# Two late copies of z, octet 7: GpSimd's queue in place of SyncE's

## The chip, the cores and the metric

The kernel runs on one core of one Trainium2 chip. The metric is device time in microseconds (us) of one execution. "TensorE" is the profile's PE (its weight loads PEld), "VectorE" DVE, "ScalarE" ACT, "GpSimd" POOL, "SyncE" SP.

## The reference

Linear attention (8 batches, 8 heads, 576 positions, head size 64) is followed by a spectral mixing block on the 512 channels:

```python
X = np.fft.rfft(x, axis=1)                      # x: the attention's output, (8, 576, 512)
Xr, Xi = (np.real(X[:, :64]), np.imag(X[:, :64]))
Yr = np.einsum('bmd,mde->bme', Xr, w_r) - np.einsum('bmd,mde->bme', Xi, w_i)
Yi = np.einsum('bmd,mde->bme', Xr, w_i) + np.einsum('bmd,mde->bme', Xi, w_r)
Y[:, :64] = Yr + 1j * Yi
y = np.fft.irfft(Y, n=576, axis=1)
u = x + y
return (u + np.maximum(u @ w_ch, 0.0)).astype(np.float32)
```

The 64 modes have a weight matrix of 512 x 512 each, real and imaginary. They are streamed in eight octets (o = 0 to 7).

## The kernel before

For each octet the kernel forms `yst` (the mixed spectrum) and `zst` (the same times `w_ch`), both 128 x 512 in bf16, and copies them by DMA into tables from which the inverse transform is taken as matmuls. Octets 6 and 7 go into `yl`, the "late" table: 16 rows of it for each copy, y into rows 0 and 64 (plus 16 for octet 7), z into rows 32 and 96.

```python
def put(src, o, dst, copies):
    if o < 7:
        sp.dma_start(dst[16 * o:16 * o + 16], src)
    if o > 5:
        for s in copies:
            r = 32 * s + 16 * (o - 6)
            (pool if o == 6 else sp).dma_start(yl[r:r + 16], src)
...
put(yst, o, yall, (0, 2))
...                                   # transposes, product with w_ch
act.copy(zst[:, cut[0]], pz[0])
dve.tensor_copy(zst[:, cut[1]], pz[1])
put(zst, o, zall, (1, 3))
```

After the last octet the output is summed in 20 steps (`seq`). The first four need only `yst` and `zst`; from step 4 on, matmuls read `yl` ("late"):

```python
def late(self, which):
    if self.early:
        return
    for a, (bp, n) in enumerate(self.items):
        r = 64 * a + 32 * which
        back((self.q if which else self.p)[a], n, bp, CL, yl, slice(r, r + 32), ...)
...
seq[2].relu()
seq[0].store()                        # ofr, 256 KB
seq[1].store()                        # ofr, 256 KB
seq[3].base(1)
seq[3].straight(1)
seq[2].store()                        # of, 512 KB
...
for g in range(3, len(seq)):
    s, ts = seq[g], [seq[i] for i in ahead[g - 3:g - 2]]
    for t in ts:
        t.base(1)
        t.straight(1)
    if g > 3:
        s.base(0)
        s.straight(0)
    for t in ts:
        t.late(1)                     # reads z from yl: the first to wait for the copies
    s.late(0)
    for t in ts:
        t.relu()
    s.store()
```

While a late matmul of TensorE waits for its copy (0.25 us before), no matmul that stands after it in the program is carried out. So a wait of the first `late(1)` holds up what TensorE has to do after it.

Of the kernel before, what the change touches and what calls it, by code (L numbers as in the profile page):

```python
# [43 lines left out]
def kernel(  # L44
# [15 lines left out]
    pool, sp = InOrder(tc, nc.gpsimd), InOrder(tc, nc.sync)  # L60
# [364 lines left out]
    for t in range(3):  # L425
        r = slice(32 * t, 32 * t + 32)
        dve.tensor_scalar_mul(out=minus[r], in0=ident_f[r, r], scalar1=-1.0)
    every = mf[0:96, 0:32]
    for t in range(3):
        r = slice(32 * t, 32 * t + 32)  # L430
# [160 lines left out]
    zall = pw.tile([128, B_, DMODEL], BF16, name="zall", tag="wt")  # L591
    yall = pw.tile([128, B_, DMODEL], BF16, name="yall", tag="wt")
    yl = pw.tile([128, B_, DMODEL], BF16, name="yl", tag="wt")
# [222 lines left out]
# [3 lines that stand above are left out]
        if o > 5:  # L819
            for s in copies:  # L820
                r = 32 * s + 16 * (o - 6)
                (pool if o == 6 else sp).dma_start(yl[r:r + 16], src)


    class Last:
# [97 lines left out]
    while mixq:  # L923
        key = mixq.pop(0)
        g, o, i = key[0], key[1] // 2, key[1] % 2
# [17 lines left out]
        if g == NG - 1 and i == 1:  # L943
# [5 lines left out]
            for h in range(2):  # L949
                dve.tensor_tensor(out=yst[:, H * h:H * h + H], in0=py[:, H * h:H * h + H],  # L950
                                  in1=yacc[:, o, H * h:H * h + H], op=ALU.add)
            put(yst, o, yall, (0, 2))
            if o < 5:
                fill(min(n, 1))
# [23 lines left out]
# [3 lines that stand above are left out]
            fill(max(n - 2, 0) if o < 5 else n)  # L981
        else:
# [70 lines left out]
```

## Time and profile before

| before | us |
|---|---|
| device time at first, median of 3 (range) | 442.57 (441.81 to 443.12) |
| span of the profiled run | 440.2 |
| last mix matmuls begin ("mix" below; the last weight tile landed just before) | 404.17 |
| end of VectorE's part of zst, octet 7 ("zst" below) | 407.66 |
| second late matmul of TensorE begins | 412.13 |
| last sum on VectorE ends | 434.82 |

Two clocks: *after mix* counts from the start of the last mix matmuls, *after zst* from the end of VectorE's `zst`. Before, the second late matmul begins 7.96 us after mix, and the second copy has landed 4.42 us after zst (412.08 - 407.66).

The page's list of DMA issues has one line for each kind of copy (source and destination, queue, count, KB, median us from issue to landing). Those of octet 7 on SyncE:

```profile
yl<-yst SPq DMA_DIRECT2D x2, 128.0 KB, 3.6
yl<-zst SPq DMA_DIRECT2D x2, 128.0 KB, 3.6
```

So a copy lands some 3.6 us after its issue has begun, of which the issue itself takes 0.55 to 0.60.

### The profile page before, as it was taken

The numbers are of one execution on the slowest core, as the hardware profiler recorded it, in microseconds if no ns is written. First come the engines' busy times: TensorE is split into PE (matmuls) and PEld (weight loads), VectorE is DVE, ScalarE is ACT, GpSimd is POOL, SyncE is SP. The second block draws the span as 40 slices with busy tenths as digits, with TensorE's granted clock in tenths as the row PEclk, the third lists the DMA queues.
The fourth block names the chain that finished last, engine by engine and source line by source line (L and its number), as shares of the span: only waits on it lengthen the run. The fifth ranks groups of instructions, "written<-read, shape, count | busy, mean of one in ns | idle before, by whom it ended". The sixth has DMA issues, their size and how long they took to land.

```text
span 440.2 us, 10147 instructions
## 1 busy us (share of the span) xinstructions
PE 337.2 (77%) x4233; PEld 203.5 (46%) x4233; DVE 296.3 (67%) x583; ACT 279.8 (64%) x478; POOL 112.5 (26%) x151
## 2 busy tenths in 40 slices
PE   1677778688688687797796787474679998998993
PEld 0445556455465465464564554252335454333320
DVE  5568686765886876976858878443883334785684
ACT  2787686786987885875857867310644442765772
POOL 6232132113211222221222221121101111682082
PEclk9978796789998896996979988975999999999997
DMA  8999999999999999999999999999999999996787
GB/s 188 211 210 211 235 215 237 231 219 239 236 210 239 221 228 235 237 212 237 228 220 238 210 237 210 238 213 210 212 216 222 222 220 220 209 219 146 251 358 294
DMA packets 51710, 99.55 MB, mean 226 GB/s; under 512 B 2512, under 2 KB 13648, under 8 KB 51664
## 3 DMA queue, kind: packets, MB, share of 16 engines
q0 software_dynamic: 45232, 85.86, 99.5%
q1 hardware_dynamic: 6432, 13.04, 8.5%
q8 instruction: 33, 0.54, 0.4%
q14 instruction: 13, 0.11, 0.1%
HBM read 163.64 MB, written 9.44 MB: 393 GB/s over the span
## 4 chain that ended last, share of the span: by engine, by line
PE 35%; DMA 25%; ACT 17%; DVE 16%; issue 5%; POOL 0%; SPq 0%; ACTq 0%; DVEq 0%; POOLq 0%
PE one L37 14%; DMA wt<-in_moe_w_i_dram 14%; PE pt L37 13%; DMA wt<-in_moe_w_r_dram 8%; ACT AB L37 7%; PE two L37 7%; DVE m L37 5%; DVE mk L37 4%; ACT AQ L37 4%; ACT XT L37 2%; DMA qb<-in_q_dram 2%; PE pp L37 2%; ACT qT L37 1%; DVE xw L37 1%; DVE XT L37 1%
## 5 line engine op out<-in xcount | busy, mean ns | idle before, releaser
L37 ACT ACTIVATE AB<-two 128x1024 bf16<-128x1024 f32 x64 | 62.0, 1026 | 11.1 <-DVE mk L37 7.8
L37 ACT ACTIVATE AQ<-two 128x1024 bf16<-128x1024 f32 x64 | 62.6, 1045 | 1.9 <-PE two L37 1.8
L37 ACT CAST xw<-pt 128x512 bf16<-128x512 f32 x50 | 29.3, 587 | 41.8 <-PE pt L37 41.7
L37 DVE TENSOR_REDUCE m<-two 128x8 f32<-128x1024 f32 x32 | 39.2, 1224 | 15.4 <-PE two L37 15.2
L37 DVE TENSOR_TENSOR va<-vn,ee 128x1152 bf16<-128x1152 f32 x32 | 42.0, 1355 | 6.3 <-DMA vn<-in_v_dram 6.2
L37 DVE TENSOR_REDUCE mk<-two 128x8 f32<-128x1024 f32 x32 | 38.9, 1218 | 9.9 <-PE two L37 9.9
L37 POOL DMA_DIRECT2D wt<-in_moe_w_i_dram x28 | 20.9, 748 | 90.2 <-PE pt L37 36.2
L37 POOL DMA_DIRECT2D wt<-in_moe_w_r_dram x30 | 22.5, 750 | 67.3 <-PE one L37 39.8
L37 PE MATMUL pt<-wchb,xT 128*128 128x512 bf16 x136 | 35.8, 387 | 5.0 <-DVE xT L37 3.8
L37 ACT COPY qT<-one 128x512 bf16<-128x512 bf16 (+1 forms) x32 | 19.5, 641 | 29.4 <-PE one L37 28.9
L37 PE MATMUL two<-w2blk,qT 128*128 128x256 bf16 x128 | 22.2, 302 | 20.0 <-ACT AQ L37 8.4
L37 PEld LDWEIGHTS <-xs 128*128 128x128 bf16 x624 | 31.3, 102 | 12.6 <-issue 7.4
L37 PE MATMUL one<-wt,XT 128*32 128x512 bf16 x304 | 28.3, 464 | 5.2 <-DMA wt<-in_moe_w_i_dram 3.6
L37 PEld LDWEIGHTS <-qT 128*128 128x128 bf16 x144 | 14.7, 104 | 36.8 <-issue 32.9
L37 PE MATMUL two<-qT,w2blk 128*128 128x512 bf16 x64 | 28.0, 438 | 3.6 <-ACT AQ L37 3.5
L37 PEld LDWEIGHTS <-AQ 128*128 128x128 bf16 x512 | 26.6, 114 | 8.7 <-issue 5.4
L37 PE MATMUL one<-kvz,AQ 128*128 128x65 bf16 x512 | 29.2, 216 | 0.9 <-ACT qT L37 0.8
L37 DVE RECIPROCAL rd<-one 128x6 f32<-128x6 f32 x48 | 9.4, 196 | 28.8 <-PE one L37 28.7
L37 DVE COPY xT<-pt 128x512 bf16<-128x512 bf16 x36 | 17.0, 471 | 17.4 <-PE pt L37 17.4
L37 PEld LDWEIGHTS <-XT 128*32 128x32 bf16 x512 | 14.7, 149 | 28.9 <-issue 22.0
L37 PE MATMUL two<-mT,minus 96*128 96x512 bf16 x64 | 28.1, 439 | 0.0
L37 DVE TENSOR_TENSOR xs<-one,rd 128x384 bf16<-128x384 f32 x48 | 26.8, 558 | 1.6
(151 smaller groups left out, 726.9 us busy)
## 6 DMA issues: line engine op xcount, KB each, us to landing
wt<-in_moe_w_r_dram POOLq DMA_DIRECT2D x30, 1024.0 KB, 28.2
wt<-in_moe_w_i_dram POOLq DMA_DIRECT2D x28, 1024.0 KB, 28.7
out_dram<-of SPq DMA_DIRECT2D x16, 512.0 KB, 4.3
vn<-in_v_dram POOLq DMA_DIRECT2D x14, 576.0 KB, 25.0
kb<-in_k_dram POOLq DMA_DIRECT2D x16, 288.0 KB, 21.0
qb<-in_q_dram POOLq DMA_DIRECT2D x16, 288.0 KB, 19.4
xs<-in_moe_w_i_dram POOLq DMA_DIRECT2D x2, 1024.0 KB, 23.7
vn<-in_v_dram SPq DMA_DIRECT2D x2, 576.0 KB, 6.8
```

What stands on the lines that cost most here:

```text
L37: ins = f(*args, **kwargs)
```

## The change

SyncE issued y's copies, then z's, then the first stores. The change sends the two z copies of octet 7 by GpSimd, which is idle then, with the intent that they don't queue on SyncE.

```diff
             for s in copies:
                 r = 32 * s + 16 * (o - 6)
-                (pool if o == 6 else sp).dma_start(yl[r:r + 16], src)
+                (pool if o == 6 or dst is zall else sp).dma_start(yl[r:r + 16], src)
```

## The prediction

> **What bounds the kernel now.** I read the page's queue table first, then the chain that ended last, then the timeline of the last 50 us, then the transfers of that stretch in short windows. For some 400 us the kernel is fed by one stream, the weights and inputs that GpSimd issues (queue table of the page; packets, MB, share of 16 engines' span):
>
> ```profile
> q0 software_dynamic: 45232, 85.86, 99.5%
> q1 hardware_dynamic: 6432, 13.04, 8.5%
> ```
>
> The change touches nothing there. Up to the eighth octet (numbered 0 to 7 in the program, so the last is o = 7) the order of every engine is the same. What counts is the end, after the last weight tile has landed at 404.12 us. The chain of waits of that stretch (start us, length us, what):
>
> ```profile
> 369.40 34.72 DMA wt<-in_moe_w_i_dram
> ...
> 407.37 0.30 DVE zst L37
> 407.67 0.02 SPq L37
> 407.69 0.03 issue
> 407.72 0.55 SPq L37
> 408.27 0.04 issue
> 408.31 3.77 DMA yl<-zst
> 412.08 0.04 issue
> 412.13 0.92 PE pt L37 x3
> ```
>
> So z of octet 7 is ready at 407.67, SyncE (SP) spends 0.55 us on issuing its first copy, then starts the second, and that one lands 3.77 us later at 412.08. The page's chain runs through it: the two copies are on the path that sets the end. How much they cost there is less than 3.77 us, since the TensorE works meanwhile. Its timeline and its weight loads show the true stall:
>
> ```profile
> 410.96 0.59 PE L37 MATMUL pt<-xw,CF 128*128 128x512 bf16 x2
> 411.49 0.09 PEld L37 LDWEIGHTS <-CL 32*128 32x128 bf16 x1 [0.42 <-DMA yl<-zst]
> 411.49 0.39 PE L37 MATMUL pt<-yl,CL 32*128 32x512 bf16 x1
> 412.12 0.09 PEld L37 LDWEIGHTS <-CL 32*128 32x128 bf16 x1 [0.55 <-DMA yl<-zst]
> 412.13 0.39 PE L37 MATMUL pt<-yl,CL 32*128 32x512 bf16 x1 [0.25 <-DMA yl<-zst]
> ```
>
> The first copy (rows 32 to 47) is in time within about 0.1 us, the second (rows 96 to 111) makes TensorE idle for 0.25 us. A matmul of 512 columns follows its predecessor every 0.215 us here, so the two late matmuls could have gone at about 411.4 and 411.6; the wait costs roughly 0.5 us of start time (412.13 against 411.6). There is no slack: **every tenth by which the second copy lands later is a tenth by which TensorE resumes later.** From there to 431 us TensorE has no gap that the timeline marks: a windows table gives 10.00 of 10 us busy for 420 to 430 at a granted clock of 1.00, and the waits of this stretch name neither VectorE nor stores as what stops it until 431.5. So a later start moves the end.
>
> **What the Trainium skill says.** (1) "DMA: Bandwidth & Descriptors", section "Latency and other measured facts": the first byte of a transfer issued by SyncE comes after about 600 ns, of one issued by GpSimd after about 1 us, because the GpSimd cores write the descriptors in software. The trace agrees in direction and has longer times. SP's z copies were issued at 407.72; no packet moved in 408.4 to 408.8 except 3 tiny ones, and they begin at about 408.93: 1.2 us. For GpSimd there is one issue onto an empty queue, the first of the kernel: issued at 1.27 for 0.86 us, and the first q0 packets fall into the window 3.8 to 4.0, so 2.6 us after the start and 1.75 us after the end of the issue (a cold start, a larger transfer, with a cast). (2) The same page, section "Issuing engines are not separate DMA queues": issuing on several engines saves only sequencer time, the 16 engines being the same. Here that time is worth nothing, see below. (3) "SBUF — State Buffer", the box on "The 'DVE blocks DMA' trap (SWDGE)": some VectorE copies lock GpSimd out of writing descriptors. I don't expect it: VectorE's work from 407.37 to 412.5 reads PSUM (zst, ofr, of), and the octet 6 copies took 0.53 us each while VectorE was busy too.
>
> **The change part by part.** The order listing shows two of SP's 28 rows leaving it and two entering GpSimd's, between its last xw sum and its first rx sum; TensorE, VectorE and ScalarE keep their order, and the first late weight loads wait for the GpSimd copies' semaphores. GpSimd is idle there: its last xw sum ends at 399.28 and its rx sum starts at 418.29, so nothing stands in front of the copies or is pushed by them. Their semaphore lanes were last used by weight tiles used at 390.66 and 394.86, so no wait comes from that.
>
> *Removed from SP:* two issues of 0.55 and 0.60 us, 407.72 to 408.91. SP's next work is the store of ofr at 409.14, which waits for VectorE (408.42 + 0.65 = 409.07). Gain: 0.
>
> *Step A, start of the issue.* Octet 6 does both at once. There zst was ready at 386.57 + 0.29 = 386.86:
>
> ```profile
> 385.57 1.11 POOL L37 DMA_DIRECT2D yl<-yst  x2 [0.20 <-PE pt L37]
> 386.57 0.29 DVE L37 CAST zst<-pt 128x128 bf16<-128x128 f32 x1 [0.94 <-PE pt L37]
> 386.92 0.55 SPq L37 DMA_DIRECT2D zall<-zst  x1
> 387.42 1.05 POOL L37 DMA_DIRECT2D yl<-zst  x2 [0.73 <-ACT zst L37]
> ```
>
> SP starts 0.06 us after it, GpSimd 0.56 us, though its own previous issue had ended at 386.68. So GpSimd should start at about 407.66 + 0.56 = 408.22 instead of 407.72: **+0.5 us**. The second issue follows after 0.53 us (408.75), on SP after 0.59 (408.31).
>
> *Step B, first packet.* SP: 1.2 us after the start. GpSimd: with the skill's difference of 0.4 us it would be 1.6 us, so packets from 409.8; with the one sample, 1.75 us after the end of the issue (408.75), 410.5. I take 410.1 against 408.93, so A and B together **+1.2 us** (B alone +0.7).
>
> *Step C, company on the engines.* On SP the first copy moves from 408.93 to about 409.55 nearly alone; the second from 409.6 to about 410.7, its end already beside the first store (issued at 409.14, moving from 410.4). Started at 410.1, both copies meet that store and its twin, 256 KB each. What full engines do to such a copy is seen in octets 0 to 6: SP's 128 KB copies beside the weight stream land after 6.6 us in the median, against 3.6 alone. Two stores are far less than the stream (and come on the other queue, with which packets alternate): an estimate of **+0.3 us** of those 3.0.
>
> Sum for the second landing: 0.5 + 0.7 + 0.3 = 1.5 us, so 413.6 instead of 412.08. Given back: TensorE's stall lets ScalarE and VectorE finish what they hold, but both are ahead of TensorE at that point (ScalarE idles 0.68 us before 411.91, VectorE 1.5 us before 414.00), so I allow 0.1. **Net +1.4 us: 442.57 + 1.4 = 444.0.**
>
> **The rivals.**
> 1. *Freed SP, or two queues at once, make it faster.* For it: the chain names 0.55 us of SP issue, and two issues could run on two engines. Against: both z copies move together, so they still queue behind each other, and the y copies had been issued by 406.9, 0.8 us before z was ready. The most that can be won is the stall, about 0.5 us: 442.1. This needs GpSimd to be quicker than SP, against steps A and B.
> 2. *A cheap switch.* GpSimd starts promptly (the 0.5 us of octet 6 being a matter of its two earlier issues) and has only the skill's 0.4 us more latency: the landing moves by 0.4 to 0.6 us, 443.0 to 443.2, within the spread of the runs of before (441.81 to 443.12).
> 3. *A dear switch.* The kernel's first issue is typical (2.6 us) and the copies meet the stores fully: 0.5 + 1.4 + 0.8 = 2.7 us, 445.3.
> 4. *The delay is hidden.* Stores keep the transfer engines at shares of 0.94 to 1.02 from 424 to 436 us; if they bound the end with a backlog, a late TensorE would cost nothing. Against: rates fall to zero at about 416 and to 40 GB/s at about 421, so no backlog reaches back to 412, and the last stores still land in about 4 us. Then 442.6.
>
> **Range and chances.** Rivals 2 and 3 span +0.4 to +2.7; with 0.3 us of run-to-run spread, 8 in 10 lie between 442.7 and 445.4, centre 444.0. Two per cent are 8.9 us: none of the mechanisms reaches that. Within 2%: 0.97; slower by more: 0.02 (only if GpSimd were locked out of its descriptors for long); faster by more: 0.01.
>
> **What would show it.** Step A: the z copies' issues in GpSimd's timeline start 0.4 to 0.6 us after the end of VectorE's zst, against 0.06 now. Step B: in short windows after them, q0 packets start 1.6 to 2.5 us after the issue's start. Step C: q0 and q1 packets share the windows, and the copies' time to landing is 4.4 to 5.3 us instead of 3.5 to 3.8. The path: the stall before the first late matmuls is about 1.7 us in place of 0.25, put down to yl<-zst, and all that follows, to the last store, is later by the same. I am wrong if the stall shrinks or keeps its size, if the end does not move with it, or if the time moved for a reason before 404 us.

## The result, and the profile after

Ratios are the mean time of one kernel's fast runs over the mean of the other's fast runs of the same rounds, so not quite the ratio of the medians quoted.

| | before | changed |
|---|---|---|
| median (range), 4 runs each | 442.73 (441.81 to 443.12) | 443.15 (442.65 to 443.82) |
| ratio, 95% interval | | 1.0014 (0.9993 to 1.0034) |
| span of the profiled run | 440.2 | 441.4 |
| last mix begins | 404.17 | 405.69 |
| second late matmul, after mix | 7.96 | 8.15 |
| last sum on VectorE ends, after mix | 30.65 | 30.99 |
| from there to the end of the span | 5.38 | 4.72 |

The spans differ by 1.2 us, and this is the first thing to read rightly: 1.52 us of it had come about before the last mix began, where both programs are the same, and 0.66 us was given back in the landing of the last stores. What the change can touch, the stretch from zst on, is longer by 0.19 us at the second late matmul and by 0.34 us at the last sum, which jitters (30.83 us after mix in the repeat).

The chain that ended last, changed kernel (start us, length us, what):

```profile
371.09 34.56 DMA wt<-in_moe_w_i_dram
...
408.62 0.49 ACT zst L37
409.11 0.64 issue
409.75 0.52 POOL yl L37
410.27 3.52 DMA yl<-zst
413.80 0.05 issue
413.84 0.92 PE pt L37 x3
```

The step that was "SPq" is now "POOL yl". It begins 0.56 us after the end of zst at 409.19 (408.90 + 0.29), as the prediction's step A had it, but the second copy then needs only 3.52 us to land, where SyncE's needed 3.77. It has landed 4.61 us after zst in place of 4.42.

The timeline of the changed kernel around it (start us, us, engine line operation, in brackets the idle time before it and what ended it):

```profile
408.90 0.29 DVE L37 CAST zst<-pt 128x128 bf16<-128x128 f32 x1 [1.07 <-PE pt L37]
409.75 1.05 POOL L37 DMA_DIRECT2D yl<-zst  x2 [8.95 <-ACT zst L37]
413.02 0.09 PEld L37 LDWEIGHTS <-CL 32*128 32x128 bf16 x1 [0.42 <-DMA yl<-zst]
413.84 0.09 PEld L37 LDWEIGHTS <-CL 32*128 32x128 bf16 x1 [0.73 <-DMA yl<-zst]
413.84 0.38 PE L37 MATMUL pt<-yl,CL 32*128 32x512 bf16 x1 [0.44 <-DMA yl<-zst]
```

The first late matmul goes as early as before (7.33 us after mix, 7.32 before). The second finds TensorE idle for 0.44 us in place of 0.25: the stall grew by 0.19 us, not by 1.4.

The queue table shows what the switch did to the packets (packets, MB, share):

```profile
q0 software_dynamic: 45328, 86.12, 99.6%
q1 hardware_dynamic: 6144, 12.78, 8.2%
```

q1 lost 6432 - 6144 = 288 packets, q0 won 45328 - 45232 = 96, for the same two copies: 144 packets each on SyncE, 48 on GpSimd. A short window at the start of each kernel's z copies shows why. Before, 408.8 to 409.2:

```profile
DMA packets 45, 0.05 MB, mean 115 GB/s; under 512 B 0, under 2 KB 45, under 8 KB 45
```

Changed, 410.8 to 411.2:

```profile
DMA packets 23, 0.09 MB, mean 236 GB/s; under 512 B 0, under 2 KB 0, under 8 KB 23
```

SyncE's copy moves in packets of 1 KB (128 of them, and 16 tiny ones under 512 B), GpSimd's in packets of 4 KB (32, and 16). Split finer, these windows give the first packets: before at about 408.93, which is 1.27 us after zst and 1.2 us after the start of the issue; changed at about 410.86, which is 1.67 us after zst but only 1.1 us after the start of the issue. Windows as fine at the other end give the last packets of the second copy: about 410.72 before and 412.43 changed, 3.06 and 3.24 us after zst. So in both kernels 1.37 us pass from the last packet to the landing, and the two copies together move for 1.79 us on SyncE's queue and for 1.57 us on GpSimd's.

### The profile page after: what moved, and what is told of

The parts are those of the page before. It is cut to its first block, busy times and chain, and to the rows that moved or that the text cites. A ratio compares the mean times of both kernels' runs of the same rounds, so it can differ in the third digit from the quotient of the medians.

```text
span 441.4 us, 10147 instructions
## 1 busy us (share of the span) xinstructions
PE 334.4 (76%) x4233; PEld 201.0 (46%) x4233; DVE 296.7 (67%) x583; ACT 279.6 (63%) x478; POOL 113.7 (26%) x153
## 3 DMA queue, kind: packets, MB, share of 16 engines
q0 software_dynamic: 45328, 86.12, 99.6%
q1 hardware_dynamic: 6144, 12.78, 8.2%
HBM read 163.64 MB, written 9.44 MB: 392 GB/s over the span
## 4 chain that ended last, share of the span: by engine, by line
PE 36%; DMA 25%; ACT 17%; DVE 16%; issue 5%; POOL 0%; ACTq 0%; DVEq 0%; POOLq 0%
PE pt L37 14%; DMA wt<-in_moe_w_i_dram 14%; PE one L37 14%; DMA wt<-in_moe_w_r_dram 8%; PE two L37 7%; ACT AB L37 7%; DVE m L37 5%; DVE mk L37 5%; ACT AQ L37 3%; ACT XT L37 2%; DMA qb<-in_q_dram 2%; PE pp L37 2%; DVE XT L37 1%; ACT qT L37 1%; DVE xw L37 1%
## 5 line engine op out<-in xcount | busy, mean ns | idle before, releaser
L37 PE MATMUL pt<-wchb,xT 128*128 128x512 bf16 x136 | 36.7, 394 | 4.7 <-DVE xT L37 3.4
L37 PE MATMUL one<-va,AB 64*128 64x65 bf16 x1024 | 22.6, 199 | 9.4 <-DVE va L37 9.4
L37 PEld LDWEIGHTS <-AQ 128*128 128x128 bf16 x512 | 25.3, 110 | 8.5 <-issue 5.0
L37 PE MATMUL one<-kvz,AQ 128*128 128x65 bf16 x512 | 27.9, 211 | 1.2 <-ACT qT L37 0.8
L37 POOL DMA_DIRECT2D kb<-in_k_dram x16 | 11.5, 720 | 64.7 <-PE one L37 54.5
```

The source lines that it names most:

```text
L37: ins = f(*args, **kwargs)
```

## The experiments

Kernels are compared only within the same rounds. All outputs are right. What the traces showed, on the two clocks (the landing is read from the start of the matmul that waited, less the 0.05 us that lie between in the chain; the last column is the start of the last but one sum on VectorE, the latest landmark that does not jitter from trace to trace):

| run | zst after mix | issue of z after zst | late matmuls after mix | second landing after zst | last but one sum, after mix |
|---|---|---|---|---|---|
| before | 3.49 | SyncE 0.06 | 7.32, 7.96 | 4.42 | 29.04 |
| before, again | 3.50 | SyncE 0.07 | 7.34, 8.01 | 4.46 | 29.09 |
| changed | 3.50 | GpSimd 0.56 | 7.33, 8.15 | 4.61 | 29.23 |
| changed, again | 3.49 | GpSimd 0.56 | 7.32, 8.14 | 4.60 | 29.22 |
| y on GpSimd, z on SyncE | 3.49 | SyncE 0.08 | 7.33, 8.09 | 4.55 | 29.17 |
| y and z on GpSimd | 3.49 | GpSimd 0.56 | 7.33, 8.12 | 4.58 | 29.19 |
| one z copy on each | 3.49 | 0.57 and 0.07 | 8.14, at once | 4.60 (first) | 29.23 |
| SyncE and ScalarE | 3.49 | 0.07 and 0.08 | 7.33, 7.97 | 4.43 | 29.05 |
| stores later, SyncE | 3.49 | SyncE 0.07 | 7.33, 7.96 | 4.42 | 29.04 |
| stores later, GpSimd | 3.49 | GpSimd 0.57 | 7.33, 8.12 | 4.58 | 29.20 |
| wait hidden, SyncE | 3.50 | SyncE 0.06 | no stall | - | 28.99 |
| wait hidden, GpSimd | 3.49 | GpSimd 0.57 | no stall | - | 28.99 |
| two dummies ahead, SyncE | 3.50 | SyncE 1.29 | 9.44, 10.22 | 6.67 | 33.94 |
| two dummies ahead, GpSimd | 3.50 | GpSimd 1.61 | 9.28, 10.77 | 7.22 | 33.35 |

Three theories were at stake. **Theory 1:** GpSimd's late start and the longer first-byte time of its queue are one and the same delay, which the prediction counted twice; the copies otherwise travel as fast. **Theory 2:** the first trace was lucky, as a rule the copies meet the stores and land a microsecond later. **Theory 3:** what TensorE wins or loses here is made up for by the stores at the end.

### The changed kernel once more

The same file, five rounds.

> The changed kernel itself once more, for five rounds. Theory 1 (the software queue's late start and its longer first-byte time are one and the same 0.4 us, which the prediction counted twice): the second z copy lands 4.5 to 4.7 us after VectorE's end of zst (4.42 before), TensorE's second late matmul starts 8.1 to 8.2 us after the last mix begins (7.96 before), and the time is 0.1 to 0.4 us longer than before. Theory 2 (the first trace was lucky, the copies as a rule meet the first stores and land 1 us later or more): the landing is 5.2 us or more after zst, the matmul starts 8.8 us or more after the mix, the time is longer by 1 us or more.

Measured: 441.65 us median against 441.76, ratio 0.9992 (0.9975 to 1.0009). Landing 4.60 us after zst, second late matmul 8.14 after mix, and the stall again 0.44 us:

```profile
411.41 0.38 PE L37 MATMUL pt<-yl,CL 32*128 32x512 bf16 x1 [0.44 <-DMA yl<-zst]
```

Theory 2 falls: two traces agree to 0.01 us. The time was expected 0.1 to 0.4 us longer and came out 0.1 shorter, within an interval of 1.5 us: device time can't resolve this effect.

### The kernel before once more

The null test: the same program on both sides.

> The kernel before against itself, to see how far two identical programs part in five rounds and how far the landing differs from one trace to the next. All theories: ratio within 0.9985 to 1.0015. Theory 1: its second z copy lands 4.3 to 4.6 us after zst and the second late matmul starts 7.9 to 8.1 us after the last mix begins; if that span overlaps the 8.14 and 8.15 of the two traces of the changed kernel, the two queues can't be told apart by landing at all. Theory 2 does not bear on it.

Measured: 442.64 us against 442.78, ratio 1.0000 (0.9979 to 1.0021). Landing 4.46 us after zst, second late matmul 8.01 after mix. Two equal programs leave an interval of 0.4%, 1.9 us. The two traces of before stand 0.05 us apart at the late matmul, those of the changed kernel 0.01, and the kernels part by 0.13 to 0.19. So the traces tell the two kernels apart and device time doesn't. (The two kernels with later stores, below, part alike: landings 4.42 and 4.58 us after zst.)

### y on GpSimd, z on SyncE

```diff
-                (pool if o == 6 else sp).dma_start(yl[r:r + 16], src)
+                (pool if o == 6 or dst is yall else sp).dma_start(yl[r:r + 16], src)
```

> y of octet 7 goes on GpSimd's queue and z stays on SyncE, as before. The y copies have empty engines. Theory 1: they start 0.5 us after yst, their first packets come 1.6 to 1.7 us after yst, they land 3.2 to 3.6 us after the start of their issue, since company played no part; z on SyncE lands after 4.4 us as before, TensorE resumes 7.9 to 8.0 us after the last mix, the time is that of before within 0.3 us. Theory 2: y on empty engines lands clearly earlier after its issue than z did in the changed kernel (2.5 us or less against 3.2 to 3.5).

Measured: 441.42 us against 441.76, ratio 0.9991 (0.9972 to 1.0010). GpSimd's y copies began 0.29 us after yst (not 0.5), their first packets came 1.4 us after yst and 1.1 after the start of the issue, they landed after 3.2 and 3.8 us:

```profile
405.34 1.05 POOL L37 DMA_DIRECT2D yl<-yst  x2 [5.91 <-DVE yst L37]
```

No store and no other copy was about, and yet the copies did not land sooner after their issue than z's in the changed kernel (3.2 and 3.5). So company on the engines was no part of what z needed there. z on SyncE landed 0.1 us later than before, a small miss. With it SyncE's spread is 4.42 to 4.55 and GpSimd's 4.58 to 4.61: the difference between the queues is hardly larger than what moving y does.

### All four copies on GpSimd

```diff
-                (pool if o == 6 else sp).dma_start(yl[r:r + 16], src)
+                pool.dma_start(yl[r:r + 16], src)
```

> All four copies of octet 7 on GpSimd's queue. Theory 1: GpSimd has finished issuing y (1.1 us from 0.5 us after yst) before zst is ready, so z starts 0.5 us after zst again and lands 4.5 to 4.8 us after it; time as the changed kernel within 0.3 us. If the 0.5 us of start is the waking of an idle GpSimd (nine microseconds without work), z starts earlier here, 0.1 to 0.3 us after zst, since GpSimd had worked 1 us before, and lands 0.3 us earlier.

Measured: 441.56 us against 441.76, ratio 0.9989 (0.9972 to 1.0007).

```profile
405.32 1.05 POOL L37 DMA_DIRECT2D yl<-yst  x2 [5.72 <-DVE yst L37]
407.61 1.05 POOL L37 DMA_DIRECT2D yl<-zst  x2 [1.24 <-ACT zst L37]
```

z's issue begins at 407.61, 0.56 us after zst (406.76 + 0.29 = 407.05), as if y's issue had not ended 1.24 us before. So the 0.56 us are not the waking of an engine that had been idle for nine microseconds.

### One z copy on each queue

```diff
-                (pool if o == 6 else sp).dma_start(yl[r:r + 16], src)
+                (pool if o == 6 or dst is zall and s == 1 else sp).dma_start(yl[r:r + 16], src)
```

> The first z copy (rows 32 to 47) on GpSimd's queue, the second (rows 96 to 111) on SyncE, so that none waits for the other's issue. Theory 1: the SyncE copy lands 3.5 us after 0.06 us, so 3.6 us after zst; the GpSimd one 0.56 + 3.2 = 3.8 us after zst. Both are there before TensorE asks (it asks 3.8 us after zst): the stall before the second late matmul is 0.0 to 0.1 us in place of 0.25 and it starts 7.3 to 7.5 us after the mix (7.96 before). If all of that reaches the end the time is 0.4 to 0.6 us shorter than before. Theory 3 (what TensorE loses or wins at this point is made up by the stores at the end): TensorE resumes as early, and the time does not move.

Measured: 441.85 us against 441.76, ratio 1.0008 (0.9987 to 1.0028). A clear miss: the late matmuls were expected at 7.3 to 7.5 us after mix, they came at 8.14, both together.

```profile
407.96 0.53 POOL L37 DMA_DIRECT2D yl<-zst  x1 [8.55 <-ACT zst L37]
412.04 0.39 PE L37 MATMUL pt<-yl,CL 32*128 32x512 bf16 x2 [0.74 <-DMA yl<-zst]
```

The first late matmul reads the copy that GpSimd made, and this needed 4.0 us from its issue, against 3.2 for the first copy in the changed kernel. In the windows, SyncE's copy moved from about 408.7 to 409.5 and GpSimd's from 409.2 to 410.6, 1.4 us where the first copy of the changed kernel took 0.7. They shared the engines for 0.3 us only: from 409.6 to 410.0 GpSimd's packets were alone, and moved 113 GB/s. Two queues let the issues run side by side, but the copy that moved second was slow, and it landed 4.60 us after zst, no sooner than with both on one queue (4.42 to 4.61). That is what the Trainium skill says ("DMA: Bandwidth & Descriptors", section "Issuing engines are not separate DMA queues"): issuing on several engines saves only the time of issuing.

### SyncE and ScalarE

```diff
-                (pool if o == 6 else sp).dma_start(yl[r:r + 16], src)
+                (pool if o == 6 else act if dst is zall and s == 3 else sp).dma_start(yl[r:r + 16], src)
```

> The first z copy on SyncE, the second on ScalarE's queue, both issued within 0.1 us of the end of zst. By the split run, in which the two copies shared the engines and the GpSimd one took 4.0 us to land, the copies should share them again, but both from 1.27 us after zst on, so that they are through before the first store moves (2.7 us after zst): both land 3.8 to 4.1 us after zst, the second late matmul starts 7.4 to 7.6 us after the mix. Against it: ScalarE loses 0.55 us to the issue just when it has the first relus to do (0.2 to 0.5 us of slack), which may delay those. Rival: the two issues take turns at one generator, and the second copy lands after 4.4 us as before.

Measured: 442.36 us against 442.78, ratio 0.9990 (0.9970 to 1.0009). Both issues began within 0.08 us of zst; SyncE's copy landed after 3.5 us, ScalarE's after 4.4, the second late matmul came at 7.97. In the windows SyncE's packets start at about 409.47, ScalarE's from 409.6 to 410.0 on, so the second did get under way, but then 59 packets of it filled the engines for the whole of 410.0 to 410.4. Landing together was expected and did not happen; whether the issues take turns at a generator or the packets at the engines, this run doesn't tell.

### The first stores issued later

The first two stores go out after the third, 2 us later, so that nothing else is on the engines while z travels.

```diff
-    seq[0].store()
-    seq[1].store()
+    held_out = [seq[0].store(), seq[1].store()]     # the sum; the DMA is held
     seq[3].base(1)
     seq[3].straight(1)
     seq[2].store()
+    for put_out in held_out:
+        put_out()
```

With z on SyncE:

> z on SyncE as before, but the first two stores (ofr, 256 KB each) are issued after the third (of), some 2 us later, so that no store is on the engines while the z copies travel. Theory 1a (before, the second z copy travels beside the first store, and the GpSimd queue, whose copies are through before that store moves, is spared this): the second copy lands 3.9 to 4.1 us after zst in place of 4.42 and 4.47, the second late matmul starts 7.5 to 7.7 us after the last mix in place of 7.96 and 8.01. If it lands after 4.4 us or more, the store is not what slows the second SyncE copy. What follows on VectorE is 0.1 to 0.4 us earlier unless the relus or banks hold it back; the time is within 0.5 us of before.

With z on GpSimd:

> The same with z on GpSimd's queue. Theory 1a: nothing changes against the changed kernel, since its z copies met no store: landing 4.5 to 4.65 us after zst, second late matmul 8.1 to 8.2 us after the last mix. If it falls by 0.3 us or more as for SyncE, the stores slowed both and theory 1a is wrong.

Measured: SyncE 441.66 us, GpSimd 441.01, against 441.72; ratios 0.9996 (0.9979 to 1.0013) and 0.9992 (0.9969 to 1.0016). Neither landing moved: 4.42 and 4.58 us after zst. For SyncE that is a miss: I had thought that its second copy was slowed by the first store, since their packets overlap. With the store out of the way the window 409.6 to 410.0, in which the second copy moves alone, shows

```profile
DMA packets 53, 0.05 MB, mean 131 GB/s; under 512 B 2, under 2 KB 53, under 8 KB 53
q1 hardware_dynamic: 53, 0.05, 125.9%
```

that is, packets that fill the engines' time (a share above 100% comes from packets that overlap) at 131 GB/s. The second copy is slow by itself; why, stays open. It is not a matter of its rows: in the run with one copy on each queue the copy into the lower rows moved second, and there that one was slow. For GpSimd theory 1 holds: without the store nothing changes. In the changed kernel the last packets of z (to 412.43) do stand beside the first packets of the store (from 411.97), so the expectation's "met no store" was not quite so, but this cost nothing that shows (4.58 against 4.60 and 4.61).

### The wait hidden behind other matmuls

TensorE gets four matmuls of the next steps before the first late ones, 0.86 us of its work.

```diff
-        for t in ts:
-            t.base(1)
-            t.straight(1)
-        if g > 3:
+        if g != 4:
+            for t in ts:
+                t.base(1)
+                t.straight(1)
+        if g == 3:
+            seq[5].base(1)
+            seq[4].base(0)
+        if g > 4:
             s.base(0)
             s.straight(0)
```

With z on SyncE:

> z on SyncE as before, but TensorE is given four matmuls of the next steps (base of q of step 5 and of p of step 4) ahead of the first late ones, 0.86 us of its work, which hides the wait. Theory 1: no stall put down to yl<-zst; the late matmuls start 8.1 to 8.3 us after the last mix begins, and all that follows is 0.4 to 0.6 us earlier, since the four matmuls need not be done later; from the last mix to the end of the last ofr on VectorE 30.1 to 30.4 us against 30.65. Time 0.3 to 0.6 us shorter than before. Theory 3 (the stores make up for it): that stretch stays at 30.6 to 31.0.

With z on GpSimd:

> The same four matmuls ahead, with z on GpSimd's queue as in the changed kernel. Theory 1: z lands 4.5 to 4.7 us after zst, which is 8.0 to 8.2 after the mix began, so nothing waits for it or 0.1 us at most, and the stretch from the last mix to the last ofr equals that of the SyncE version within 0.15 us: the queue no longer matters at all. Theory 2: a stall of 0.4 us or more remains.

Measured: SyncE 442.99 us, GpSimd 442.08, against 442.78; ratios 1.0011 (0.9989 to 1.0034) and 0.9985 (0.9963 to 1.0006). No wait for `yl<-zst` is left in either, and the last but one sum comes at 28.99 in both: with the wait hidden the queue makes no difference, as theory 1 has it. The gain over before is 0.05 to 0.10 us, though, where 0.4 to 0.6 was expected. TensorE's waits in the SyncE version from 7 us after mix on name what took the stall's place:

```profile
PE pt L37 <- ACT rl L37: 0.5, 1, 0.5
```

The relus of step 4 on ScalarE begin only when the late matmuls are done, and the next step's matmuls need the PSUM banks that they free. Whether this wait would have come anyway is not shown: with four matmuls put ahead, the relus of step 4 begin 8.62 us after mix in place of 7.74, so that the new order may itself have made it. The two versions' medians differ by 0.9 us at equal landmarks, which is the noise again; their last sums end 30.60 and 30.82 us after mix.

### Two dummy copies ahead

Two further copies of z into a buffer that is no longer read go in front of the two that count, on the same queue.

```diff
+        if o == 7 and dst is zall:
+            spill = XTb[0]...                 # as (128, 8, 512)
+            for s in (0, 2):
+                sp.dma_start(spill[32 * s:32 * s + 16], src)      # pool in the other kernel
         if o > 5:
             for s in copies:
```

On SyncE:

> Two more copies of z, into a buffer that nobody reads any more, go on SyncE ahead of the two that count. Landing later by two issues of 0.6 us and the engines' 1.2 us of transfers: 5.6 to 5.8 us after zst, second late matmul 9.1 to 9.4 us after the last mix (7.96 and 8.01 before). Theory 1 (TensorE's resuming sets what follows): the sums on VectorE that follow, up to the first of the last two ofr, are later by the same 1.1 to 1.4 us. Theory 3: later by less than half of it.

On GpSimd:

> The same two dummy copies on GpSimd's queue ahead of the two that count. Two issues of 0.53 us: landing at least 1.1 us later than in the changed kernel, so 5.7 us after zst, second late matmul 9.2 us or more after the last mix. Now the copies that count move at the same time as the first stores. If company costs as the prediction's step C had it (0.3 us): 9.4 to 9.6. If it costs next to nothing: 9.2 to 9.3. Theory 1: VectorE's later sums move by the same amount as the matmul.

Measured: SyncE 445.90 us, GpSimd 445.35, against 441.72; ratios 1.0090 (1.0068 to 1.0111) and 1.0081 (1.0051 to 1.0111). These are the only runs that device time tells from before. Both landed later than the issues explain: SyncE's second late matmul is 2.2 us later than before (7.96 to 8.01), GpSimd's 2.6 us later than in the changed kernel. Here the copies that count did meet the stores: GpSimd's two took 4.1 and 5.1 us from issue to landing in place of 3.2 and 3.5. So company, of the stores and of the dummies ahead on the same queue, which the run doesn't separate, cost up to 1.6 us here.

And the last but one sum was later by 4.9 us (SyncE) and 4.1 us (GpSimd), more than the matmul that waited. The windows of the SyncE run (window, its length, busy us of the engines with the count of instructions, granted clock, DMA share, GB/s) show why:

```profile
410.00:412.00 2.00, 0.68 (x4) 0.10 (x1) 1.54 (x2) 0.35 (x1) 0.00 (x0) 1.00 1.18 121
412.00:413.00 1.00, 0.28 (x1) 0.09 (x1) 0.00 (x0) 0.00 (x0) 0.00 (x0) 0.94 0.95 221
413.00:414.00 1.00, 0.71 (x2) 0.10 (x1) 0.00 (x0) 0.60 (x1) 0.00 (x0) 0.50 1.08 424
...
418.00:419.00 1.00, 1.00 (x6) 0.24 (x6) 0.01 (x1) 0.14 (x1) 0.00 (x0) 0.50 0.00 0
419.00:420.00 1.00, 1.00 (x4) 0.30 (x2) 1.00 (x1) 0.94 (x2) 0.00 (x0) 0.65 0.92 381
420.00:421.00 1.00, 1.00 (x8) 0.21 (x6) 0.48 (x2) 0.40 (x1) 0.00 (x0) 1.00 0.35 143
```

After a stall of 2.04 us the granted clock fell to half at about 412.9 and stayed there until 419.7, although TensorE was busy throughout from 414 on. Pairs of matmuls that take 0.60 us before took 1.03:

```profile
412.72 0.49 PE L37 MATMUL pt<-yl,CL 32*128 32x512 bf16 x1 [2.04 <-DMA yl<-zst]
413.50 0.60 PE L37 MATMUL pt<-yl,CL 32*128 32x512 bf16 x1 [0.29 <-DMA yl<-zst]
414.03 1.03 PE L37 MATMUL pt<-xw,CF 128*128 128x512 bf16 x2
```

Theory 3 falls: a delay at this point reaches the end, and a long one reaches it enlarged. In the GpSimd run the clock stood at 1.00 through a first stall of 1.88 us and fell at about 414.8, at the end of a second one of 1.10 us; it returned at 418.2. So its late matmul came 0.55 us later than the SyncE run's (10.77 against 10.22), and its last but one sum 0.59 us earlier (33.35 against 33.94): 3.4 us at half clock in place of 6.8.

None of these versions is shown faster than the kernel before. The hidden wait is the only one whose landmarks are earlier (by up to 0.1 us), less than device time resolves.

## Why the prediction was right or wrong

The measured 443.15 us lies in the predicted range (442.7 to 445.4), and the change was put within 2%, as it is. The direction in the trace was right too. The size was not: net +1.4 us was predicted, and the late matmul moved by 0.13 to 0.19 us. So it is partly luck that the time lies in the range: 442.57 plus 0.13 to 0.19 is 442.70 to 442.76, the range's lower edge, and the spread of the runs did the rest. Of the signs that the prediction named, step A's came true (0.56 us). Step B's (1.6 to 2.5 us from issue to first packet, measured 1.1), step C's (4.4 to 5.3 us to landing, measured 3.2 and 3.5) and the path's (a stall of 1.7 us, measured 0.44) did not.

- **The path** was read rightly: the two z copies stand in the chain, the second late matmul waits for the second copy, and from before to changed the landing, the matmul (by 0.13 to 0.19) and the last but one sum (29.04 and 29.09 to 29.22 and 29.23) move by the same amount. "A tenth later is a tenth later" held for this shift; with the dummies ahead the sums moved by more than the matmul. The wait's cost was read too low: the first late matmul starts 7.32 to 7.34 us after mix wherever its copy is there, and when both copies are there the two start together (412.04, x2, with one copy on each queue). So the second was held up by an estimated 0.64 us before (7.96 - 7.32) and not by 0.5. What landing earlier would win is not shown: no run landed z earlier, and hiding the wait won 0.05 to 0.10 us, with another wait in its place. So rival 1 stays open as to what there is to win.
- **Removed from SyncE, gain 0:** right. The issue of the first store begins 1.48 us after zst in both kernels.
- **Step A, start of the issue, +0.5 us:** right, 0.56 us against 0.06, in every trace with z on GpSimd alone or after y. "The second issue follows after 0.53" was right too (0.52), which gives back 0.07 against SyncE's 0.59.
- **Step B, first packet, a further +0.7 us: this is the term that failed.** From the recorded start of its issue, GpSimd's first packet takes 1.1 us, SyncE's 1.2: the term is -0.1. The prediction took the skill's 0.4 us of longer first-byte time, and more from the kernel's first issue, and added it to the late start. Counted from the moment that the data is ready, the trace has 1.67 against 1.27 us: 0.4 us in all, which is the skill's difference, once. The Trainium skill, "Perfetto Trace Analysis", sections "DMA Instruction — HWDGE (DVE, Sync)" and "DMA Instruction — SWDGE (GPSIMD)", would have warned of it: for SyncE's issue the recorded start is the moment when all semaphores are satisfied, while GpSimd's has no start marker, only the end of descriptor writing. The trace does print a start for GpSimd's, but the two are not the same event, and a part of GpSimd's latency lies before its own. The traces agree as far as the sum goes; no run shows what fills the 0.5 us, except that it isn't the waking of an idle engine, and that y's issue began 0.29 us after its data and not 0.56. (y is written by VectorE alone, z by ScalarE and VectorE, so z's issue waits for two engines; no run tests whether that is the difference.)
- **The kernel's first issue as a measure** (2.6 us to the first packet) misled: the same queue needed 1.1 us here, for y and for z.
- **Step C, company, +0.3 us:** zero here. Without the 0.7 of step B only the last packets of GpSimd's second copy (from 411.97 to 412.43) meet the store's, and the kernel without a store there lands within 0.03 us of this one. As a price of company the term may have been too small: with dummies ahead, company of both kinds cost up to 1.6 us.
- **The sum:** +0.50 (start) - 0.07 (second issue) - 0.25 (3.52 in place of 3.77 us from the second issue to landing) = +0.18, against 4.61 - 4.42 = 0.19 measured. By packets it reads more simply: the first is 0.40 us later after zst, the two copies move for 1.57 us in place of 1.79, and 1.37 us from the last packet to the landing are the same: 0.40 - 0.22 = 0.18. The shorter move goes with packets of 4 KB; that it comes from them is argued, not shown.
- **The measured +0.4 us of the medians** (443.15 against 442.73) is not confirmed as the effect of the change: the repeat has -0.1, the null test an interval of 0.4%. What the traces support is 0.13 to 0.19 us at the second late matmul, 0.03 to 0.04% of the time.

## What to carry to other kernels

When a transfer moves to another queue, compare from the moment its data is ready to the moment its reader may start; recorded starts of issues on different engines need not be the same event, and terms measured from them may be counted twice. When an effect is a thousandth of the time, compare landmarks after a common event inside the trace, and run the kernel against itself once, so as to know what the time can tell. And before a wait is valued, ask what would hold the engine next, and what the wait's length does to the clock: here 0.44 us did nothing to it, and in the run with 2.04 us it stood at half for 6.8 us.

## What the Trainium skill lacked or had wrong

- "DMA: Bandwidth & Descriptors", "Latency and other measured facts": the first-byte times of about 0.6 us (SyncE) and 1 us (GpSimd) are given without saying from when. Here they were 1.27 and 1.67 us from the readiness of the data, 1.2 and 1.1 us from the recorded start of the issue. The difference of 0.4 holds for the first reading alone.
- The same page, "SWDGE vs HWDGE vs iDMA", gives packets of preferably no more than 4096 B for the software queue. It doesn't say that the hardware queue splits the same copy otherwise: here 128 packets of 1 KB and 16 tiny ones on SyncE, 32 of 4 KB and 16 tiny ones on GpSimd, for 128 KB of rows of 1 KB.
- "TensorE: Matmul & The Clock Gate", "Part 1: The HAM clock gate", has the clock fall after at least one idle window of about 3.4 us. Here it fell to 0.50 after less: 2.04 us of marked idle time before one late matmul (and 1.88 and 1.10 us with one matmul between in the other run), and it took 6.8 us to return in one run (412.9 to 419.7, with one gap of 0.29 us in the work), 3.4 us (414.8 to 418.2) in the other: two and one of the page's windows.
- No page has the 0.56 us (z) and 0.29 us (y) from the readiness of the data to the recorded start of GpSimd's issue.
